# Bounce stores queued one by one behind weight loads, and the leftover tokens' first product with both halves of x side by side

## The chip, the cores and the metric

The kernel runs on 1 core of a Trainium2 chip. The metric is the device time of one execution in microseconds. Before the change the median of 3 runs is 1294.83 us (1294.04 to 1295.26).

The engines are named as in the profile: PE (matrix multiplies; PEld is its weight load), DVE (vector), ACT (scalar), POOL (GpSimd) and SP, which only issues DMAs. All DMAs of this kernel are issued by SP, and its rows in the trace are rows of issuing.

## The reference

A linear-attention layer, then a feed-forward layer, then four dense experts weighted by probabilities, on 2304 tokens of 512 features:

```python
def phi(x):
    proj = np.einsum('bhsd,df->bhsf', x, w_phi)
    proj = proj - np.max(np.abs(proj), axis=-1, keepdims=True)
    return np.concatenate([np.exp(proj), np.exp(-proj)], axis=-1)
q_p, k_p = (phi(q), phi(k))
kv = np.einsum('bhsf,bhsd->bhfd', k_p, v)
z = np.sum(k_p, axis=2)
x = einsum(q_p, kv) / (einsum(q_p, z) + 1e-6)      # 2304 x 512
...
h = x @ w_in                                       # 2048 wide
x = (h * (1.0 / (1.0 + np.exp(-1.702 * h)))) @ w_out
...
p = domain_probs / (domain_probs.sum(-1, keepdims=True) + 1e-09)
for e in range(4):
    out += p[:, e:e + 1] * (np.maximum(x @ w1[e], 0.0) @ w2[e])   # 1024 wide
```

## The kernel before, in words

**Tokens and units.** The tokens are held feature-major in SBUF in two groups: group 0 of 1024 tokens and group 1 of 1280, which is two halves of 512 and a REST of 256 "leftover tokens". Each feed-forward layer is cut into units, each a slab of 256 hidden columns. The list UNITS runs through them: units 0 to 7 are layer 1 on group 0, 8 to 15 layer 1 on group 1, 16 to 31 layer 2 on group 0, 32 to 47 layer 2 on group 1 (these are in LATE). NU is 8. Numbers are split into a high and a low part in a matmul format, and each product takes three matmuls (PASSES): weights high with x high, weights high with x low, weights low with x high.

**A unit.** For the 1024 tokens in halves a unit makes seven block products (steps 0 to 6, function first and products, 6 matmuls of 512 columns each); the second products of the unit before are put between the steps. The PSUM banks 0, 1 and 2 ("a", "b", "c") take the first products: bank 0 from step 0 on, bank 2 from step 5 on. The 256 leftover tokens take no part in the blocks: in units of group 1, rest_first is called after step 3 (its result in bank 2) and after step 5 (in bank 0), and each time plain_rest makes 12 matmuls of 256 columns (4 slices of the features, 3 passes). Then hidden() makes the activation: in layer 1 a tanh gate by ACT (L778), a multiply by DVE (L781), a cast by ACT (L793) and the low part by POOL; in layer 2 a relu by ACT (L797) and the low part by DVE (L798). Over the program plain_rest runs 48 times: 2 times for each of 8 units of layer 1 and 16 of layer 2.

**Two ways in which the order is set.** The attention stage and the units 0 to 8 are one list of words, ORDER, written out by hand; in_order ties each instruction to the one before it on its engine. From unit 9 on a loop over UNITS writes the rest, with background work (generators in the list bg, one step per call) between the steps. SP is not held to ORDER: the scheduler places a DMA where it finds it ready.

**The attention stage, as far as the change touches it.** Each of the 16 pairs of heads takes a maximum over the features; it goes to DRAM (rd1, mx_d, L615) and comes back broadcast to all partitions (rd2, "mb", L620). The subtraction of it (es, L625) and the two exponentials (en L628, ep L631) make the pair's eq, which the matmuls n0 to n2 (L703, 72 rows) read. The key side has exponentials too (kn L670, kp L673), read by the matmuls v0 and v1 (L678, L685). Between them the layer-1 weights, which come as 64-bit numbers, are loaded (h..ld, raws, L266) and converted (abs L338, rb L340, sg L344, cl L346, sh L350, ad L352, mu L354 or L358) and stored to w1_d for the second group (st, L323), from where load() reads them again (L290).

**The probabilities.** They are loaded into pn and normalised (np0, np1; L512 to L517). For units 32 to 47 a row of them is needed along the free axis, so each expert's 1024 values of group 1 are written to pn_d in DRAM (L1356: 128 partitions, 8 values of 4 bytes each) and read back broadcast (row, L314) from unit 32 on. The four stores stand in the loop at unit NU + 2, that is 10, and nothing ties them to a place on SP.

Of the kernel before, what the change touches and what calls it, by code (L numbers as in the profile page):

```python
# [9 lines left out]
F32 = mybir.dt.float32  # L10
F32R = mybir.dt.float32r
# [7 lines left out]
P = 128  # L19
# [4 lines left out]
KC = DM // P  # L24
F1 = 2048 // P
E = 4
F2 = 1024 // P
NG = F1 + E * F2
PASSES = ((0, 0), (0, 1), (1, 0))

HALF = 512
BASE = (0, 1024)
SIZE = (1024, 1280)
REST = SIZE[1] - 2 * HALF
# [9 lines left out]
NU = 8  # L44
# [115 lines left out]
def fused(ctx: ExitStack, tc: tile.TileContext, qT, kT, v, w_phi, wg1, wg2, probs, out):  # L160
    nc = tc.nc
# [33 lines left out]
    def bank(i, n=1):  # L195
        return psa[:, i * 512:(i + n) * 512]

    TAGS = ("a", "b", "c", "acc0", "acc1", "acc2", "acc3", "acc4")
# [9 lines left out]
    pn_d = dram.tile([E, 8, P], F32, name="pn_d")  # L208
# [12 lines left out]
    def low(eng, dst, src, hi):  # L221
        eng.tensor_tensor(out=dst, in0=src, in1=hi.bitcast(F32), op=ALU.subtract)  # L222


    raw64, raw, win, wout = {}, {}, {}, {}
# [12 lines left out]
    late = {}  # L238
# [7 lines left out]
    def third_area():  # L246
        leave("A")
        pool = enter("D")
        for i in (2, 4, 5):
            late["xo%d" % i] = pool.tile([P, 2, 2, HALF], F32R, name="xo%d" % i)  # L250
        late["ss"] = pool.tile([P, 4, 256], F32, name="ss")
        late["xr"] = [pool.tile([P, KC, REST], F32R, name="xr%d" % e) for e in range(2)]
        ring["gr"] = deque(pool.tile([P, 2, REST], F32R, name="gr%d" % i) for i in range(2))
        late["mm"] = pool.tile([P, HALF], F32, name="mm")
        late["uu"] = pool.tile([P, 2, HALF], F32, name="uu")
        late["h"] = pool.tile([P, HALF], F32, name="hs")
        late["id"] = pool.tile([P, P], F32, name="ident_out")
# [55 lines left out]
    def row(e, k):  # L313
        nc.sync.dma_start(  # L314
            out=prow(k), in_=pn_d[e, 4 * k:4 * k + 4].rearrange("t p -> (t p)").rearrange("(o n) -> o n", o=1)
            .to_broadcast([P, HALF])
        )

    def prow(k):
        return late["ss"].rearrange("p (a b) f -> p a (b f)", a=2)[:, k]  # L320
# [111 lines left out]
    xo = {}  # L432
# [50 lines left out]
    def build_rest():  # L483
        xo["rest"] = t = late["xr"]
        src = xv[1][:, :, 2 * HALF:]
        nc.scalar.copy(t[0], src)
        yield
        low(nc.vector, t[1], src, t[0])
        yield

    bg = deque()
# [366 lines left out]
    class Unit:  # L858
# [97 lines left out]
                self.psf[0, 1] = self.c  # L956

        def plain_rest(self, i, ps):
            k_ = 0
            for kc in range(KC):  # L960
                for a, e in PASSES:
                    nc.tensor.matmul(  # L962
                        ps, win[self.u][:, a, 2 * i + kc // 2, (kc % 2) * P:(kc % 2 + 1) * P], xo["rest"][e][:, kc, :],
                        start=(k_ == 0), stop=(k_ == 11),
                    )
                    k_ += 1

        def plain_first(self, i, k, ps):
            n = 0
# [14 lines left out]

        def rest_first(self, i, tag):
            older, self.stages = self.stages, deque()
            ps = bank(TAGS.index(tag))[:, :REST]
            self.plain_rest(i, ps)
            self.g[i, 2], st = hidden(self.layer, ps, REST)
            next(st)  # L990
            self.stages.append(st)
            self.finish(older)
# [136 lines left out]
    def ffn(name, slot, var):  # L1129

        kind = name.rstrip("0123456789.")
        u, *ij = (int(x) for x in name[len(kind):].split("."))
        unit = units.setdefault(u, Unit(u))
        if kind in "PMUBHC":
            unit.strassen_step(kind, *ij, slot)
            return
        i, j = ij
        if kind in "SE":
            if kind == "S":
                unit.sums[i, j] = bank(int(slot[1:]))  # L1140
                unit.plain_second(i, j, unit.sums[i, j])
            else:
                unit.plain_add(i, j, unit.sums[i, j])
        elif kind == "F":
            unit.psf[i, j] = bank(int(slot[1:]))
            if j == 2:
                unit.plain_rest(i, unit.psf[i, j][:, :REST])
            else:
                unit.plain_first(i, j, unit.psf[i, j])
        else:  # L1150
            n = REST if j == 2 else HALF
            src = unit.psf[i, j][:, :n]
            if kind == "Va":
                unit.sg[i, j] = sgs[int(slot)][:, :n]
                gate(unit.sg[i, j], src)
            sg = unit.sg[i, j]
            if kind == "Vb":
                gated(sg, src)
            elif kind == "Ha":
                unit.g[i, j] = ring["gr"][int(slot)] if j == 2 else gs[int(slot)]  # L1160
                nc.scalar.copy(unit.g[i, j][:, 0, :], sg)
            elif kind == "Hb":
                g = unit.g[i, j]
                low(nc.vector if var else nc.gpsimd, g[:, 1, :], sg, g[:, 0, :])
# [151 lines left out]
    for u, (grp, layer, q) in list(enumerate(UNITS))[NU + 1:]:  # L1316
        unit = Unit(u)
        if u + 5 < len(UNITS) and UNITS[u + 5][2] == 0:
            ready = deque(build_x(UNITS[u + 5][0], (3, 6)).values())
        if u + 1 < len(UNITS) and UNITS[u + 1][2] == 0:  # L1320
            while pre:
                pump(pre)
            bx = ready
        if u in LATE:
            if u + 1 < len(UNITS):
                bg.append(load_in(u + 1))
            if u == LATE[0]:
                last_stage()
            else:
                bg.append(chain(before))  # L1330
            if u == LATE[-2]:
                bg.appendleft(gather((4, 7)))
            if u == LATE[-1]:
                bg.append(gather((6, 1), (4, 6), (2, 1)))
            bg.append(prep_out(u))
            if u != LATE[-1]:
                bg.append(prep_sums_out(u))
            bg.append(load(u + 2))
        else:
            if layer == 2:  # L1340
                bg.append(sums_out(u))
            else:
                bg.append(prep_sums(u + 1))
            bg.append(prep_out(u))
            bg.append(load(u + 2))
            if u + 1 in LATE:
                bg.append(load_in(u + 1))
            else:
                if layer == 2:
                    bg.append(prep_sums(u + 1))  # L1350
                bg.append(prep_in(u + 1))
                if UNITS[u + 1][1] == 2:
                    bg.append(store_in(u + 1))
        if u == NU + 2:
            for e in range(E):
                nc.sync.dma_start(out=pn_d[e].rearrange("t p -> p t"), in_=pn[:, BASE[1] // P:BASE[1] // P + 8, e])  # L1356
        if grp and q == 0:
            for _ in build_rest():
                pass
        strassen_unit(unit)  # L1360
        while bg or free:
            background(1)
        unit.finish(unit.stages)
        before = unit
# [54 lines left out]
```

## Time and profile before

| | before |
|---|---|
| median of 3 runs | 1294.83 us |
| the profiled execution | 1290.59 us, of which 1288.8 us lie between its first and last instruction (the span) |
| PE busy | 1259.6 us (98%) |
| PEld, DVE, ACT, POOL busy | 1054.6, 810.8, 538.6, 799.0 us |
| granted TensorE clock, mean | 0.992 of full speed |
| PE busy in 40 slices of the span | 8999999967999999999999999999999999999999 |

A digit of the last row is the busy share of one slice in tenths (9 is 90% or more); a slice is 1288.8 / 40 = 32.2 us long. PE is busy nearly throughout; the slices that fall out are the ninth and the tenth, 258 to 322 us from the start, which is the end of the attention stage. The other engines are idle for a third of the span or more, so that PE is the one to follow.

### The profile page before, as it was taken

The numbers are of one execution on the slowest core, as the hardware profiler recorded it, in microseconds if no ns is written. First come the engines' busy times: TensorE is split into PE (matmuls) and PEld (weight loads), VectorE is DVE, ScalarE is ACT, GpSimd is POOL, SyncE is SP. The second block draws the span as 40 slices with busy tenths as digits, with TensorE's granted clock in tenths as the row PEclk, the third lists the DMA queues.
The fourth block names the chain that finished last, engine by engine and source line by source line (L and its number), as shares of the span: only waits on it lengthen the run. The fifth ranks groups of instructions, "written<-read, shape, count | busy, mean of one in ns | idle before, by whom it ended". The sixth has DMA issues, their size and how long they took to land.

```text
span 1288.8 us, 20442 instructions
## 1 busy us (share of the span) xinstructions
PE 1259.6 (98%) x8181; PEld 1054.6 (82%) x8181; DVE 810.8 (63%) x1243; ACT 538.6 (42%) x826; POOL 799.0 (62%) x617
## 2 busy tenths in 40 slices
PE   8999999967999999999999999999999999999999
PEld 6888878856888888888888888888888888888887
DVE  7887777744844565655544556566466666666675
ACT  6987565644454333542222323233522322322321
POOL 5634343323776775795757567554876886787784
PEclk9999999987999999999999999999999999999999
DMA  7754544354110010244445443555334334423302
GB/s 230 227 167 143 182 157 134 113 89 97 63 66 34 33 66 34 98 164 196 158 186 204 169 200 147 212 212 199 129 132 139 137 116 136 158 104 141 147 1 82
DMA packets 62161, 174.00 MB, mean 135 GB/s; under 512 B 28018, under 2 KB 28402, under 8 KB 55922
## 3 DMA queue, kind: packets, MB, share of 16 engines
q1 hardware_dynamic: 62066, 172.70, 38.6%
q8 instruction: 64, 1.05, 0.3%
q14 instruction: 31, 0.25, 0.1%
HBM read 117.54 MB, written 55.14 MB: 134 GB/s over the span
## 4 chain that ended last, share of the span: by engine, by line
PE 71%; ACT 0%; issue 0%; ACTq 0%
PE psa L873 29%; PE psa L1037 17%; PE psa L1075 11%; PE psa L1035 8%; PE psa L962 5%; PE psa L1116 1%; PE psa L1106 0%; ACT xa L1123 0%; ACTq L1123 0%
## 5 line engine op out<-in xcount | busy, mean ns | idle before, releaser
L873 PE MATMUL psa<-xo,win 128*128 128x512 f32 x1680 | 422.4, 389 | 0.0
L873 PEld LDWEIGHTS psa<-xo,win 128*128 128x128 f32 x1680 | 314.1, 188 | 64.9 <-POOL win L222 0.3
L1037 PE MATMUL psa<-wout,g 128*128 128x512 f32 x768 | 189.7, 389 | 0.0
L222 POOL TENSOR_TENSOR g<-sg,g 128x512 fp32r<-128x512 f32 x85 | 114.0, 1345 | 105.8 <-ACT g L793 53.2
L222 POOL TENSOR_TENSOR wout<-raw,wout 128x1024 fp32r<-128x1024 f32 (+1 forms) x49 | 108.0, 2205 | 103.1 <-ACT wout L413 102.0
L1037 PEld LDWEIGHTS psa<-wout,g 128*128 128x128 f32 x768 | 144.1, 188 | 29.8
L880 DVE TENSOR_TENSOR xa<-psa,xa 128x512 f32<-128x512 f32 x178 | 119.9, 688 | 12.7 <-PE psa L1075 12.7
L1057 DVE SCALAR_TENSOR_TENSOR xa<-psa,pn,xa 128x512 f32<-128x512 f32 x114 | 85.4, 749 | 64.8 <-PE psa L1037 64.7
L222 POOL TENSOR_TENSOR g<-xa,g 128x512 fp32r<-128x512 f32 x69 | 89.2, 1299 | 31.0 <-ACT g L821 30.8
L797 ACT ACTIVATE g<-psa 128x512 fp32r<-128x512 f32 x48 | 28.7, 598 | 180.8 <-DVE psa L880 125.1
L1035 PE MATMUL psa<-g,wout 128*128 128x512 f32 x384 | 95.3, 390 | 0.4 <-DVE xa L1005 0.4
L996 PE MATMUL psa<-g,wout 128*128 128x512 f32 x384 | 92.7, 392 | 0.0
L1075 PE MATMUL psa<-g,ws 128*128 128x512 f32 x360 | 92.2, 391 | 0.0
L973 PE MATMUL psa<-xo,win 128*128 128x512 f32 x384 | 91.8, 391 | 0.0
L880 DVE TENSOR_TENSOR uu<-psa,mm 128x512 f32<-128x512 f32 x80 | 55.1, 688 | 56.3 <-PE psa L873 50.4
L973 PEld LDWEIGHTS psa<-xo,win 128*128 128x128 f32 x384 | 71.6, 188 | 15.6 <-issue 0.6
L996 PEld LDWEIGHTS psa<-g,wout 128*128 128x128 f32 x384 | 71.3, 188 | 15.8 <-DVE eq L625 0.4
L1035 PEld LDWEIGHTS psa<-g,wout 128*128 128x128 f32 x384 | 71.1, 188 | 15.0 <-DVE xa L1005 0.9
L821 ACT CAST g<-xa 128x512 fp32r<-128x512 f32 x72 | 44.7, 621 | 88.6 <-DVE xa L812 43.1
L222 POOL TENSOR_TENSOR win<-raw,win 128x1024 fp32r<-128x1024 f32 (+1 forms) x31 | 67.7, 2185 | 19.1 <-ACT win L427 12.2
L962 PEld LDWEIGHTS psa<-xr,win 128*128 128x128 f32 x576 | 75.4, 191 | 3.7
L962 PE MATMUL psa<-xr,win 128*128 128x256 f32 x576 | 76.6, 283 | 0.0
(161 smaller groups left out, 2161.5 us busy)
## 6 DMA issues: line engine op xcount, KB each, us to landing
wi_d<-win SPq DMA_DIRECT2D x16, 2048.0 KB, 6.3
win<-wi_d SPq DMA_DIRECT2D x16, 2048.0 KB, 8.1
raws<-in_wg_dram SPq DMA_DIRECT2D x32, 512.0 KB, 5.5
raw<-in_wg_dram SPq DMA_DIRECT2D x16, 1024.0 KB, 5.1
w_d<-raw SPq DMA_DIRECT2D x8, 1024.0 KB, 6.6
raw<-w_d SPq DMA_DIRECT2D x8, 1024.0 KB, 4.6
ws_d<-ss SPq DMA_DIRECT2D x16, 512.0 KB, 4.5
raw<-in_wg_dram SPq DMA_DIRECT2D x16, 512.0 KB, 3.2
```

The source lines that it names most:

```text
L222: eng.tensor_tensor(out=dst, in0=src, in1=hi.bitcast(F32), op=ALU.subtract)
L797: nc.scalar.activation(out=hi, in_=src, func=AF.Relu)
L821: nc.scalar.copy(g[:, 0], h)
L873: nc.tensor.matmul(ps, win[self.u][:, a, w, kc * P:(kc + 1) * P], xo[i][:, e, kc, :], start=start and k_ == 0, stop=stop and k_ == 5, skip ...
L880: nc.vector.tensor_tensor(out=out, in0=ps, in1=other, op=ALU.add)
L962: nc.tensor.matmul(ps, win[self.u][:, a, 2 * i + kc // 2, (kc % 2) * P:(kc % 2 + 1) * P], xo["rest"][e][:, kc, :], start=(k_ == 0), stop=( ...
L973: nc.tensor.matmul(ps, win[self.u][:, a, 2 * i + kc // 2, (kc % 2) * P:(kc % 2 + 1) * P], x[:, e, kc % 2, :], start=(n == 0), stop=(n == 11),)
L996: nc.tensor.matmul(ps, wout[self.u][:, a, i, t * P:(t + 1) * P], self.g[i, k][:, e, :], start=(n == 0), stop=(n == 5))
L1035: nc.tensor.matmul(p, w[:, a, i, t_ * P:(t_ + 1) * P], v_, **f)
L1037: nc.tensor.matmul(p, v_[:, t_ * P:(t_ + 1) * P], w[:, a, i, :], **f)
L1057: nc.vector.scalar_tensor_tensor(out=o, in0=ps, scalar=col, in1=o, op0=ALU.mult, op1=ALU.add)
L1075: nc.tensor.matmul(ps, quarter(a), g[:, e, :], start=n == 0 and (m != 5 or first), stop=n == 2 and (m != 5 or final), skip_group_check=True,)
```

## The change

**The bounce stores.** The four stores to pn_d leave the loop body of unit 10. A generator store_row(e) makes one of them and ties it behind the last SP instruction written so far; it is put into bg right behind load(u + 2), so the units 10, 11, 12 and 13 each store one expert's row behind their weight load.

**The leftover tokens.** Both parts of their x become one tile, xr, so that for one slice of the features the high part and the low part (256 columns each, 1024 elements apart) can be one moving operand of 512 columns. plain_rest then makes, for each of 4 slices, one matmul of 512 columns with the high weights and one of 256 with the low weights: 8 matmuls in place of 12, and as many columns. The results lie side by side in a whole bank, and fold() adds them: ACT copies the right 256 columns to SBUF (fold), DVE adds them to the left 256 in place. Unit 8 keeps the 12 matmuls; the other 23 units of group 1 take the new form, 46 times.

```diff
-        late["xr"] = [pool.tile([P, KC, REST], F32R, name="xr%d" % e) for e in range(2)]
+        late["xr"] = pool.tile([P, 2, KC, REST], F32R, name="xr")
+        late["fold"] = pool.tile([P, REST], F32, name="fold")
...
+    def store_row(e):
+
+        traced = nc.cur_bb.bb.instructions
+        behind = next(i for i in reversed(traced) if i.engine == mybir.EngineType.SP).name
+        start = len(traced)
+        nc.sync.dma_start(out=pn_d[e].rearrange("t p -> p t"), in_=pn[:, BASE[1] // P:BASE[1] // P + 8, e])
+        for ins in traced[start:]:
+            tc.add_manual_dep(
+                ins, behind, mybir.DependencyInfo(mybir.DependencyClass.NoSync, mybir.DependencyReason.DATA),
+                reason="step order",
+            )
+        yield
...
         def plain_rest(self, i, ps):
-            k_ = 0
+
+            x, n = xo["rest"], 0
+            if self.u == NU:
...
             for kc in range(KC):
-                for a, e in PASSES:
+                for a, w in ((0, 2 * REST), (1, REST)):
                     nc.tensor.matmul(
-                        ps, win[self.u][:, a, 2 * i + kc // 2, (kc % 2) * P:(kc % 2 + 1) * P], xo["rest"][e][:, kc, :],
-                        start=(k_ == 0), stop=(k_ == 11),
+                        ps[:, :w], win[self.u][:, a, 2 * i + kc // 2, (kc % 2) * P:(kc % 2 + 1) * P],
+                        x[:, :, kc, :] if a == 0 else x[:, 0, kc, :],
+                        start=(n == 0), stop=(n == 2 * KC - 1), skip_group_check=True,
                     )
-                    k_ += 1
+                    n += 1
+
+        def fold(self, ps):
+            nc.scalar.copy(late["fold"], ps[:, REST:])
+            self.add(ps[:, :REST], ps[:, :REST], late["fold"])
+            return ps[:, :REST]
...
         def rest_first(self, i, tag):
             older, self.stages = self.stages, deque()
-            ps = bank(TAGS.index(tag))[:, :REST]
+            ps = bank(TAGS.index(tag))
             self.plain_rest(i, ps)
+            ps = self.fold(ps)
...
             bg.append(load(u + 2))
+            if 0 <= u - NU - 2 < E:
+                bg.append(store_row(u - NU - 2))
...
-        if u == NU + 2:
-            for e in range(E):
-                nc.sync.dma_start(out=pn_d[e].rearrange("t p -> p t"), in_=pn[:, BASE[1] // P:BASE[1] // P + 8, e])
```

The scheduler's order on SP, near the end of the attention stage, before the change: the maximum of the last pair goes out (m to mx_d), comes back broadcast (mx_d to mb), the last two 64-bit weight loads follow (raws), then the stores and loads of layer-1 weights (w_d).

```order
L615 DMA mx_d<-m_123 36x32
L1356 DMA pn_d<-pn 128x8x1
L620 DMA mb_114<-mx_d 128x1152
L1356 DMA pn_d<-pn 128x8x1 x3
L266 DMA raws_0_91<-in_wg_dram 128x512
L266 DMA raws_1_92<-in_wg_dram 128x512
L323 DMA w_d<-raw_140 128x2048
```

And with the change, from the same place on:

```order
L629 DMA mx_d<-m_123 36x32
L634 DMA mb_114<-mx_d 128x1152
L267 DMA raws_0_91<-in_wg_dram 128x512
L267 DMA raws_1_92<-in_wg_dram 128x512
L337 DMA w_d<-raw_140 128x2048
L291 DMA raw_140<-w_d 128x2048
L337 DMA w_d<-raw_141 128x2048
L291 DMA raw_141<-w_d 128x2048
L291 DMA raw_140<-w_d 128x2048
L291 DMA raw_141<-w_d 128x2048
L291 DMA raw_140<-w_d 128x2048
L325 DMA pn_d<-pn 128x8x1
```

Before, one store to pn_d stands ahead of the broadcast that fills mb, and three stand between it and the loads of raws. Now the broadcast and the two loads follow each other directly. The first store to pn_d stands behind the load of unit 12's weights, five loads of raw later; the other three follow in the same way, each behind the load of the next unit's weights (13, 14 and 15).

On DVE, around the second set of leftover tokens in a steady unit of layer 1 (steps 5 and 6). Before (hs is the sum of step 5, sg_102 the gate of the leftover tokens, the xa row the eviction of a second product, the last two the value of step 6):

```order
L880 TENSOR_TENSOR hs<-psa,uu 128x512
L781 SCALAR_TENSOR_TENSOR sg_103<-sg_103,hs 128x512
L781 SCALAR_TENSOR_TENSOR sg_102<-sg_102,psa 128x256
L1049 TENSOR_TENSOR xa_75<-psa,xa_75 128x512
L880 TENSOR_TENSOR psa<-psa,uu 128x512
L781 SCALAR_TENSOR_TENSOR sg_103<-sg_103,psa 128x512
```

With the change:

```order
L894 TENSOR_TENSOR hs<-psa,uu 128x512
L795 SCALAR_TENSOR_TENSOR sg_103<-sg_103,hs 128x512
L894 TENSOR_TENSOR psa<-psa,fold 128x256
L1080 TENSOR_TENSOR xa_75<-psa,xa_75 128x512
L795 SCALAR_TENSOR_TENSOR sg_102<-sg_102,psa 128x256
L894 TENSOR_TENSOR psa<-psa,uu 128x512
L795 SCALAR_TENSOR_TENSOR sg_103<-sg_103,psa 128x512
```

The addition of the fold comes ahead of the eviction, and the last read of bank 0, the multiply of 256 columns into sg_102, moves behind it. On ACT the copy to fold takes the place of the gate of 256 columns, which follows behind the cast of the hs value. Everything before unit 9 stands on PE, ACT, DVE and POOL as before, apart from the names of the xr tiles.

## Rows read from the trace of the kernel before

**Rows 1.** Who PE waited for: engine, line, releaser: us in total, times, longest.

```profile
PE psa L703 <- ACT eq L631: 10.3, 1, 10.3
```

**Rows 2.** PE's timeline, end of attention: start, us, instruction, count, idle before and releaser.

```profile
256.65 0.44 PE L678 MATMUL psa<-v,ek 128*64 128x130 f32 x4
...
259.11 0.28 PE L607 MATMUL psa<-ident,r 128*36 128x128 f32 x1
...
272.65 6.96 PE L996 MATMUL psa<-g,wout 128*128 128x512 f32 x30
289.95 3.91 PE L703 MATMUL psa<-kv,eq 128*64 128x65 f32 x72 [10.34 <-ACT eq L631]
...
303.05 2.00 PE L685 MATMUL psa<-v,ek 128*64 128x65 f32 x32 [8.96 <-ACT ek L673]
...
307.15 0.66 PE L735 MATMUL psa<-ident,on 128*128 128x128 f32 x4
...
308.00 2.32 PE L703 MATMUL psa<-kv,eq 128*64 128x65 f32 x72
```

**Rows 3.** SP's timeline there: start and length of issuing.

```profile
267.29 0.38 SPq L1356 DMA_DIRECT2D pn_d<-pn  x1
267.77 0.52 SPq L620 DMA_DIRECT2D mb<-mx_d  x1
268.33 12.95 SPq L1356 DMA_DIRECT2D pn_d<-pn  x3
281.38 11.73 SPq L266 DMA_DIRECT2D raws<-in_wg_dram  x2
```

**Rows 4.** DVE's timeline there.

```profile
285.09 1.36 DVE L625 TENSOR_TENSOR eq<-eq,mb 128x1152 f32<-128x1152 f32 x1 [12.36 <-DMA mb<-mx_d]
```

**Rows 5.** ACT's timeline there.

```profile
286.48 2.22 ACT L628 ACTIVATE eq<-eq 128x1152 f32<-128x1152 f32 x2 [13.07 <-DVE eq L625]
288.73 1.16 ACT L631 ACTIVATE eq<-eq 128x1152 f32<-128x1152 f32 x1
301.40 0.65 ACT L344 ACTIVATE raws<-raws 128x512 f32<-128x512 f32 x1 [11.51 <-DMA raws<-in_wg_dram]
```

**Rows 6.** DMA issues by line: count, KB each, median us from issue to landing.

```profile
raws<-in_wg_dram SPq DMA_DIRECT2D x32, 512.0 KB, 5.5
...
xa<-mx_d SPq DMA_DIRECT2D x8, 576.0 KB, 4.4
```

**Rows 7.** One stretch: busy time of each engine, granted clock (PEclk), DMA share.

```profile
284.00:286.00 2.00, 0.00 (x0) 0.00 (x0) 0.91 (x1) 0.00 (x0) 0.00 (x0) 0.50 1.01 27
```

**Rows 8.** POOL's timeline, end of attention.

```profile
272.26 1.32 POOL L358 TENSOR_TENSOR raw<-raw,raws 128x512 f32<-128x512 f32 x1 [5.61 <-ACT xa L748]
```

**Rows 9.** PE's timeline in a steady unit of layer 1, group 1.

```profile
435.89 1.60 PE L962 MATMUL psa<-xr,win 128*128 128x256 f32 x12
437.32 1.55 PE L1035 MATMUL psa<-g,wout 128*128 128x512 f32 x6
438.71 2.88 PE L873 MATMUL psa<-xo,win 128*128 128x512 f32 x12
441.43 1.52 PE L1035 MATMUL psa<-g,wout 128*128 128x512 f32 x6
```

**Rows 10.** DVE's timeline there.

```profile
437.54 0.69 DVE L781 SCALAR_TENSOR_TENSOR sg<-sg,hs 128x512 f32<-128x512 f32 x1 [0.76 <-ACT sg L778]
438.15 0.41 DVE L781 SCALAR_TENSOR_TENSOR sg<-sg,psa 128x256 f32<-128x256 f32 x1
438.91 0.69 DVE L1049 TENSOR_TENSOR xa<-psa,xa 128x512 f32<-128x512 f32 x1 [0.35 <-PE psa L1035]
```

**Rows 11.** ACT's timeline there.

```profile
437.60 0.38 ACT L778 ACTIVATE sg<-psa 128x256 f32<-128x256 f32 x1
```

**Rows 12.** SP's timeline, two loads of layer-1 weights in steady units.

```profile
397.87 0.32 SPq L290 DMA_DIRECT2D raw<-w_d  x1
...
424.45 0.32 SPq L290 DMA_DIRECT2D raw<-w_d  x1
```

More of the change, by code (lines that the diff above doesn't have):

```diff
@@ L485, in build_rest @@
         src = xv[1][:, :, 2 * HALF:]
-        nc.scalar.copy(t[0], src)
+        nc.scalar.copy(t[:, 0], src)
         yield
-        low(nc.vector, t[1], src, t[0])
+        low(nc.vector, t[:, 1], src, t[:, 0])
         yield
@@ L958, in plain_rest @@
         def plain_rest(self, i, ps):
-            k_ = 0
+            x, n = xo["rest"], 0
+            if self.u == NU:
+                for kc in range(KC):
+                    for a, e in PASSES:
+                        nc.tensor.matmul(
+                            ps[:, :REST], win[self.u][:, a, 2 * i + kc // 2, (kc % 2) * P:(kc % 2 + 1) * P],
+                            x[:, e, kc, :], start=(n == 0), stop=(n == 11),
+                        )
+                        n += 1
+                return
             for kc in range(KC):
-                for a, e in PASSES:
+                for a, w in ((0, 2 * REST), (1, REST)):
                     nc.tensor.matmul(
-                        ps, win[self.u][:, a, 2 * i + kc // 2, (kc % 2) * P:(kc % 2 + 1) * P], xo["rest"][e][:, kc, :],
-                        start=(k_ == 0), stop=(k_ == 11),
-                    )
-                    k_ += 1
+                        ps[:, :w], win[self.u][:, a, 2 * i + kc // 2, (kc % 2) * P:(kc % 2 + 1) * P],
+                        x[:, :, kc, :] if a == 0 else x[:, 0, kc, :],
+                        start=(n == 0), stop=(n == 2 * KC - 1), skip_group_check=True,
+                    )
+                    n += 1
+        def fold(self, ps):
+            nc.scalar.copy(late["fold"], ps[:, REST:])
+            self.add(ps[:, :REST], ps[:, :REST], late["fold"])
+            return ps[:, :REST]
         def plain_first(self, i, k, ps):
@@ L1146, in ffn @@
             if j == 2:
-                unit.plain_rest(i, unit.psf[i, j][:, :REST])
+                unit.plain_rest(i, unit.psf[i, j])
             else:
```

## The prediction

> **What bounds the kernel now.** I read the page first: PE is busy for 98% of the span, at nearly full clock, so time is gained only where a matmul gets cheaper or where PE waits. Then the view of who PE waited for: its longest entry is one wait of 10.3 us for an exponential on ACT [rows 1]. The timeline of PE shows where: 10.34 us ahead of the n matmuls at 289.95, and a second wait of 8.96 us ahead of the v matmuls at 303.05 [rows 2]. Both lie at the end of the attention stage.
>
> Followed back, the first wait goes: PE waits for the exponentials on ACT, ACT for the subtraction L625 on DVE [rows 5], and DVE stands still for 12.36 us until the DMA that fills mb lands [rows 4]. That DMA was issued at 267.77 [rows 3], so it took 17.3 us to be used at 285.09. The same kind of transfer (xa<-mx_d, as large) lands after 4.4 us in the median [rows 6]. The second wait: ACT stood 11.51 us ahead of the sign L344 for a load of raws [rows 5], and the exponential that PE wants is queued behind that sign. SP shows what both have in common: a store to pn_d was issued 0.48 us ahead of mb, three more right behind it kept SP issuing for 12.95 us, and the two loads of raws behind those took 11.73 us more to get out [rows 3]. These stores move only 4 KB each, but as 1024 values of 4 bytes. So I read both waits as one queue blocked by the stores.
>
> The pause has a second price. At 284 to 286 the granted clock is 0.50 [rows 7], the lower of the two levels (1.2 GHz), and PE had done nothing since 279.6. The 72 n matmuls at 289.95 then take 3.91 us, where the same 72 at 308.00 take 2.32 [rows 2].
>
> **The stores moved: what it is worth.** I rebuild the stretch from the end of the 30 matmuls that start at 272.65 [rows 2]. One matmul of 512 columns goes out every (441.43 - 438.71) / 12 = 0.227 us [rows 9], so PE could go on at 272.65 + 30 x 0.227 = 279.45.
>
> First, is the n group ready by then? With mb issued at 267.77 as before and 4.4 us of landing [rows 6], it is there at 272.2. DVE is free at 285.09 - 12.36 = 272.73 [rows 4]. From the start of L625 to the first exponential are 1.39 us, from there to L631 2.25, and L631 takes 1.16 [rows 4, 5]: 272.73 + 4.80 = 277.5. That is 1.9 us before PE asks, so the first wait is gone.
>
> Second, the v group. The load of raws needs the buffer that POOL frees at 272.26 + 1.32 = 273.6 [rows 8]; with 5.5 us to landing [rows 6] the sign can start at 279.1, and PE was released 303.05 - 301.40 = 1.65 us after that start [rows 2, 5]: 280.75. PE comes there after the n matmuls, at 279.45 + 2.3 = 281.75. The margin is 1.0 us; the second wait is gone too.
>
> Then the stretch takes 2.3 us for n and 259.11 - 256.65 = 2.46 us for v, both as at full clock [rows 2]: 279.45 + 4.8 = 284.2. Before, PE reached the next matmuls (L735) at 307.15 [rows 2]. **Term 1: 22.9 us gained**, of which 19.3 are the two waits and some 3.6 the clock. What follows hangs on the same releases and moves up as a whole. In their new place the stores cost only queue time: loads of layer-1 weights follow each other by 26.6 us [rows 12], and four stores, mb and the loads together were through by 301.4 [rows 3, 5], that is (301.4 - 267.3) / 4 = 8.5 us a store at the most. A store is out of the queue long before the next load comes. Cost 0.
>
> On the order of the queue there is the Trainium skill, "DMA: Bandwidth & Descriptors", section "Two DMAs through the same engine are not ordered": descriptors of one queue start in order. The trace agrees: mb, issued behind one store, was late. [...]
>
> **The leftover tokens: what it is worth.** A set of 12 matmuls of 256 columns takes 437.32 - 435.89 = 1.43 us, 0.119 each [rows 9]. The new set is 4 of 512 and 4 of 256: 4 x 0.227 + 4 x 0.119 = 1.385. The columns are the same; what is saved is what each matmul costs beside its columns, four times. 46 sets give 46 x 0.046 = 2.1 us. The trace has no moving operand of 512 columns in two pieces. If such a matmul cost as much as two of 256 (0.239), nothing would be left; I take the row of 512, since neither a piece boundary nor its cost shows anywhere, and keep 0 to 2.1.
>
> [...] The rows say 13 ns beside the columns at 2.4 GHz (512 / 2.4 = 213 ns of 227). [...]
>
> The fold adds, 46 times, a copy on ACT (like the gate of 256 columns, 0.38 us [rows 11]) and an addition on DVE (like the multiply of 256, 0.41 [rows 10]). Neither engine is the bound. What can be late is bank 0: the next unit's step 0 writes it. Its first matmul stands 6 x 0.227 behind 438.71 [rows 9], at 440.07, or 440.02 with the shorter set. In front of that now come: end of the set 437.44, copy 437.60 to 437.98 [rows 11], DVE's multiply of hs until about 438.15, the fold's addition, the eviction, which starts at 438.91 as before (it waits for PE), 0.61 to the next instruction (437.54 to 438.15), and the multiply of 0.41 [rows 10]: 438.91 + 0.61 + 0.41 = 439.93. It just fits, where before it had 1.5 us. Behind step 3 bank 2 is free until step 5, and in layer 2 more matmuls stand between. I take 0.5 us lost over the seven units of layer 1, from bounds of 0 and 2. **Term 2: 1.6 us gained.**
>
> **The sum.** 22.9 + 1.6 = 24.5 us. On the profiled execution that is 1290.6 - 24.5 = 1266.1. That execution lies 4.2 us under the median of the runs; on the median I get 1294.8 - 24.5 = **1270.3 us**.
>
> **Rivals.**
> 1. *Another wait takes part of the stall's place.* The margin ahead of v is only 1.0 us. If the load of raws took twice as long (11 us), PE would wait 4.5 us, and v would run at the lower clock, 2 us more: 1276.8. If the second wait stayed whole (9.0 us, with the 3.6 of clock), 12.6 us come back: 1282.9. For it: ACT's queue is full of conversions that wait for these loads. Against it: 5.5 is the median with other traffic, and here the queue is empty.
> 2. *The stores are not the cause*, and mb is late for another reason. Then term 2 alone is left: 1293.2. Against it: SP's issuing of 12.95 and 11.73 us [rows 3].
> 3. *Slower:* a moving operand in two pieces streams at a lower rate. At half rate the 184 new matmuls of 512 columns cost 0.227 us more each, 41.8 us, and with term 1 (22.9) the kernel ends 17 us slower by the median, 1312 us. It decides from 24.5 / 184 = 0.133 us more each. No row speaks for it; none shows such an operand either.
>
> **How the numbers follow.** The forecast has a chance of 0.73 (1264 to 1275, with the bounds of the two terms and the 4.2 us between profile and median, should they belong to the stall), rival 1 0.16 (1275 to 1283), rival 2 0.06, rival 3 0.05. The range 1264 to 1281 holds the forecast and most of rival 1. About 0.2% (2.6 us) is what a measurement can tell from no change: rival 2 falls inside it. Faster 0.89, same 0.06, slower 0.05.
>
> **What would show it.** In the profile after, DVE waits for mb under 2 us; PE has no wait above 1 us between the L996 matmuls and L735 and the granted clock stays at full speed there; SP issues one store to pn_d behind each of four loads, 26 us apart, with nothing late behind it; a leftover set takes 1.38 us in 8 matmuls; PE waits for DVE at the start of layer-1 units by some tenths at most. The forecast falls if mb still takes over 10 us to land, if PE waits for ACT ahead of v, or if a set takes more than 1.43 us.

## The result, and the profile after

| | before | with the change |
|---|---|---|
| median | 1295.05 us (1294.04 to 1297.04, 4 runs: the three known before and one more) | 1266.2 us (1265.47 to 1267.56, 4 runs) |
| profiled execution, span | 1290.59, 1288.8 | 1265.47, 1263.7 |
| PE busy | 1259.6 us (98%) | 1252.8 us (99%) |

The ratio is 0.9777, with an interval of 0.976 to 0.9794. Forecast were 1270.3 us and a range of 1264 to 1281. The gain between the two profiled executions is 25.1 us (24.5 forecast), that between the medians 28.9.

SP's timeline of the changed kernel, at the place of [rows 3], at the first weight load that now has a store behind it, and at the next weight load (start of issuing, and the time from the first start to the last end of a merged row):

```profile
266.22 0.33 SPq L634 DMA_DIRECT2D mb<-mx_d  x1
272.63 8.60 SPq L267 DMA_DIRECT2D raws<-in_wg_dram  x2
...
373.75 0.32 SPq L291 DMA_DIRECT2D raw<-w_d  x1
374.12 0.43 SPq L325 DMA_DIRECT2D pn_d<-pn  x1
400.31 0.32 SPq L291 DMA_DIRECT2D raw<-w_d  x1
```

DVE's timeline, at the place of [rows 4]; then ACT's, at that of [rows 5]:

```profile
271.67 2.15 DVE L639 TENSOR_TENSOR eq<-eq,mb 128x1152 f32<-128x1152 f32 x1
```

```profile
273.85 2.22 ACT L642 ACTIVATE eq<-eq 128x1152 f32<-128x1152 f32 x2 [1.42 <-DVE eq L639]
276.11 1.17 ACT L645 ACTIVATE eq<-eq 128x1152 f32<-128x1152 f32 x1
277.18 0.66 ACT L358 ACTIVATE raws<-raws 128x512 f32<-128x512 f32 x1
277.74 1.04 ACT L687 ACTIVATE ek<-ek 128x1024 f32<-128x1024 f32 x1
```

PE's timeline there, the stretch of [rows 2]:

```profile
271.68 6.96 PE L1027 MATMUL psa<-g,wout 128*128 128x512 f32 x30
278.57 2.32 PE L717 MATMUL psa<-kv,eq 128*64 128x65 f32 x72
...
280.94 1.10 PE L699 MATMUL psa<-v,ek 128*64 128x65 f32 x32
...
283.13 0.66 PE L749 MATMUL psa<-ident,on 128*128 128x128 f32 x4
```

And the windows view of that stretch (busy time of PE, PEld, DVE, ACT, POOL; granted clock, DMA share, GB/s):

```profile
271.00:283.00 12.00, 12.00 (x178) 10.44 (x176) 8.01 (x14) 9.03 (x13) 7.25 (x6) 1.00 0.22 66
```

The subtraction that stood 12.36 us for mb stands for nothing, and neither does the sign that stood 11.51 us for raws: no bracket stands behind it. PE goes through without a gap at full clock. From the 30 matmuls to the transposes (L749) it takes 283.13 - 271.68 = 11.45 us, where it took 34.50. The longest wait of PE left in the whole span is 1.7 us, at 31.55, long before. PE reaches the stretch 0.97 us earlier than before. That is no work of the change: nothing ahead of the stretch was changed, and this start moves from run to run (272.28 in e1, 273.17 in e5, which repeats the changed kernel).

PE's timeline in a steady unit of layer 1, the place of [rows 9], and at the last unit of layer 1 (second piece):

```profile
411.73 1.56 PE L986 MATMUL psa<-xr,win 128*128 128x512 f32 x8
413.13 1.55 PE L1066 MATMUL psa<-g,wout 128*128 128x512 f32 x6
414.52 2.93 PE L887 MATMUL psa<-xo,win 128*128 128x512 f32 x12
417.29 1.07 PE L1066 MATMUL psa<-g,wout 128*128 128x512 f32 x4
...
519.49 3.42 PE L887 MATMUL psa<-xo,win 128*128 128x512 f32 x12
522.75 1.52 PE L1066 MATMUL psa<-g,wout 128*128 128x512 f32 x6
```

DVE's timeline in the same unit, the place of [rows 10]:

```profile
413.99 0.42 DVE L894 TENSOR_TENSOR psa<-psa,fold 128x256 f32<-128x256 f32 x1
414.72 0.69 DVE L1080 TENSOR_TENSOR xa<-psa,xa 128x512 f32<-128x512 f32 x1 [0.30 <-PE psa L1066]
415.33 0.41 DVE L795 SCALAR_TENSOR_TENSOR sg<-sg,psa 128x256 f32<-128x256 f32 x1
```

A leftover set takes 413.13 - 411.73 = 1.40 us (1.43 before; 1.385 forecast). The 12 matmuls of step 6 and the next step 0 take 417.29 - 414.52 = 2.77 in place of 2.72: the multiply that frees bank 0 ends at 415.74, and step 0's first matmul would stand at 414.52 + 1.36 = 415.88, so the fit is as tight as forecast. In unit 15 it doesn't fit, and the same twelve take 522.75 - 519.49 = 3.26.

### The profile page after: what moved, and what is told of

The parts are those of the page before. It is cut to its first block, busy times and chain, and to the rows that moved or that the text cites. A ratio compares the mean times of both kernels' runs of the same rounds, so it can differ in the third digit from the quotient of the medians.

```text
span 1263.7 us, 20113 instructions
## 1 busy us (share of the span) xinstructions
PE 1252.8 (99%) x7997; PEld 1039.9 (82%) x7997; DVE 827.5 (65%) x1289; ACT 554.6 (44%) x872; POOL 797.9 (63%) x617
## 4 chain that ended last, share of the span: by engine, by line
PE 72%; DVE 1%; ACT 0%; issue 0%; ACTq 0%; DVEq 0%
PE psa L887 29%; PE psa L1068 17%; PE psa L1106 11%; PE psa L1066 8%; PE psa L986 5%; PE psa L1147 1%; DVE xo L222 0%; PE psa L1137 0%; ACT sg L792 0%; DVE sg L795 0%; DVE xa L1080 0%; DVE psa L894 0%; DVE hs L894 0%; ACT fold L994 0%; ACT xa L1154 0%
## 5 line engine op out<-in xcount | busy, mean ns | idle before, releaser
L894 DVE TENSOR_TENSOR xa<-psa,xa 128x512 f32<-128x512 f32 x178 | 121.1, 687 | 12.7 <-PE psa L1106 12.7
L1106 PEld LDWEIGHTS psa<-g,ws 128*128 128x128 f32 x360 | 65.4, 188 | 13.7
L792 ACT ACTIVATE sg<-psa 128x512 f32<-128x512 f32 (+1 forms) x72 | 39.3, 549 | 79.5 <-PE psa L887 24.5
```

The lines of the kernel that those rows point to most:

```text
L792: nc.scalar.activation(out=out, in_=src, func=AF.Tanh, scale=0.851)
L894: nc.vector.tensor_tensor(out=out, in0=ps, in1=other, op=ALU.add)
L1106: nc.tensor.matmul(ps, quarter(a), g[:, e, :], start=n == 0 and (m != 5 or first), stop=n == 2 and (m != 5 or final), skip_group_check=True,)
```

## The experiments

The runs follow four questions. Each kernel was timed beside the kernel before on the same chip, on four chips in all. The kernel before ran there at 1290.84, 1294.52, 1291.71 and 1293.24 us (medians).

### What each half of the change is worth

**e1_stores_only**: the change without its product; every unit makes the 12 matmuls, and no fold.

```
-            if self.u == NU:
+            if True:
...
-            ps = self.fold(ps)
+            ps = ps[:, :REST]
```

> The four stores moved behind the loads as in the change, the leftover tokens' product as before (12 matmuls of 256 columns, no fold). Theory (the stores in the queue held up mb and raws; moving them is nearly the whole gain): no wait of PE above 1 us between the second products at 272 us and the transposes, a span some 1.1 us above the changed kernel's 1263.7, about 1264.8, and 28 us under before in the timed runs, about 1267.3. Rival (the new product carries a good part): 1275 or more in the timed runs.

**e2_rest_only**: the product with its fold, the stores where they were before.

```
-            if 0 <= u - NU - 2 < E:
-                bg.append(store_row(u - NU - 2))
...
+        if u == NU + 2:
+            for e in range(E):
+                nc.sync.dma_start(out=pn_d[e]..., in_=pn[...])
```

> The leftover tokens' product as in the change, the four stores where they were before. Theory: both waits of PE, 10 us and 9 us, stay; a set takes 1.40 us instead of 1.43, 46 sets give 1.5 us, some tenths go back as waits for bank 0: 1.1 us faster than before, 0.9991 of its time. Rival (the product is worth several us by itself): 0.997 or less.

**e3_before_again**: the kernel before, unchanged.

> The kernel before, unchanged, profiled once more. The profiled execution of before took 1290.6 us, its timed runs 1294 to 1297. Theory: the difference lies in the stall itself, whose length goes by how fast the stores are worked off and so varies between executions; an execution of 1295 us then has the two waits of PE longer by some 4 us together, and everything else as long as before. Rival: the 4 us lie elsewhere (the start, the loads), and the two waits are 10.3 and 9.0 us again.

**e5_after_again**: the changed kernel, unchanged, on the second chip.

> The changed kernel, unchanged, beside the kernel before on one chip and beside the stores-only kernel's times. In the first comparison before took 1295 us and the change saved 28.9, while the two profiles differ by 25.1 and the stores-only kernel saved 22.8 where before took 1290.8. Theory: the change itself always takes about 1266 to 1267 and before varies between sessions with the length of its stall; where before takes 1291 the change saves 24 to 25 (22.8 and 0.7 to 1.1 for the product), ratio 0.981. Rival: the saving is 29 on every chip, ratio 0.978.

Measured, as ratio to the kernel before: e1 1268.06 us, 0.9818 (0.9804 to 0.9833); e2 1290.13 us, 0.9992 (0.9983 to 1.0002); e3 1291.07 us, 1.0005 (0.9995 to 1.0015); e5 1266.99 us, 0.9786 (0.9772 to 0.9801). PE's timeline of e1 in the stretch, then who PE waited for in e2:

```profile
279.17 2.32 PE L717 MATMUL psa<-kv,eq 128*64 128x65 f32 x72
...
281.54 1.10 PE L699 MATMUL psa<-v,ek 128*64 128x65 f32 x32
```

```profile
PE psa L717 <- ACT eq L645: 10.1, 1, 10.1
PE psa L699 <- ACT ek L687: 9.6, 1, 9.6
```

The stores alone give 22.8 us and remove both waits; the product alone leaves both waits whole and gives 0.7 us, which is within its interval of nothing. So nearly all of the gain is the stores. e1 has the tiles of the change, too, and takes 913.7 us from the first leftover set of unit 9 to the end of the span, as the kernel before does; so a mere shift of tiles, which costs so much in e7 below, plays no part here.

Two of these runs did not settle what they were for. e3 was to show an execution of 1295 us, and its profiled one took 1290.46, no longer than the first. e5 repeats the time of the changed kernel, but ran on a chip where the kernel before takes 1294.52, so that it does not show what the change saves where that takes 1291.

### What in a store delays its neighbours

**e4_stores_of_32_bytes**: the stores stay in front, four DMAs of 4 KB each, but from a small copy in which a partition's 8 values stand together: 128 pieces of 32 bytes in place of 1024 of 4. The rows are then read back in another order, so that e4 and e6 leave out the order that the reference wants; the work and the bytes are the same.

```
-    pn_d = dram.tile([E, 8, P], F32, name="pn_d")
+    pn_d = dram.tile([E, P, 8], F32, name="pn_d")
...
+    pn_e = const.tile([P, E, 8], F32, name="pn_e")
...
-                nc.sync.dma_start(out=pn_d[e].rearrange("t p -> p t"), in_=pn[...])
+                nc.sync.dma_start(out=pn_d[e], in_=pn_e[:, e, :])
```

> The kernel before, with the four stores at their old place, but each writing 128 runs of 32 bytes from a small copy of pn in which a partition's 8 values lie together, instead of 1024 values of 4 bytes. The rows that are read back for the last 16 units hold the probabilities in another order than the reference wants. Theory (it is the count of small pieces that blocks the queue): both waits of PE are gone, the span is within 3 us of the stores-only kernel, some 1265 to 1268. Rival (four more DMAs ahead cost by their number, whatever their pieces): a wait of some us stays, 1275 or more. Second rival (the stores are not the cause): 1289 as before.

**e6_32_bytes_no_shift**: the same, with the copy in a tile that the program already has for padding, so that no other tile moves (the edit is against e4).

```
-    pn_e = const.tile([P, E, 8], F32, name="pn_e")
+    pn_e = spare_edge[:, 0:32].rearrange("p (e t) -> p e t", e=E)
```

> The kernel before with the four stores at their old place as 128 runs of 32 bytes, the small copy of pn now in a padding tile that is allocated anyway, so that no other tile moves. The rows that are read back hold the probabilities in another order than the reference wants. In the first form of this run both waits of PE were gone, but matmuls whose moving operand is xo took 0.233 us each instead of 0.227 all through the program. Theory (the copy moved all later tiles by 128 bytes, and that is what slowed those matmuls; the stall goes by the count of pieces): now the whole gain shows, 1267 to 1269, as in the stores-only kernel. Rival (something in the stores or rows slows the matmuls): 1280 again.

**e7_shift_alone**: the kernel before, with a tile of the copy's size (128 bytes a partition) that nothing uses.

```
+    const.tile([P, 32], F32, name="shift")
```

> The kernel before with nothing but an unused tile of 128 bytes a partition ahead of the later tiles. Theory (the place of a moving operand in SBUF sets what its matmuls cost beside their columns): 0.233 us for the matmuls with xo, 10 to 13 us slower than before, ratio 1.008 to 1.010, the two waits as before. Rival: no change, 1.000.

Measured: e4 1280.09 us, 0.9915 (0.9897 to 0.9932); e6 1267.03 us, 0.9787 (0.977 to 0.9803); e7 1306.13 us, 1.0087 (1.0072 to 1.0102). SP's timeline of e6:

```profile
266.55 0.33 SPq L1358 DMA_DIRECT2D pn_d<-edge  x1
266.98 0.37 SPq L622 DMA_DIRECT2D mb<-mx_d  x1
267.39 1.38 SPq L1358 DMA_DIRECT2D pn_d<-edge  x3
272.81 8.61 SPq L266 DMA_DIRECT2D raws<-in_wg_dram  x2
```

The order of the queue is that of before, and so are the bytes; SP issues three stores in 1.38 us where it took 12.95, both waits are gone, and the time is that of the stores moved away. What delays is neither the number of DMAs nor their place in the queue as such, but that each is cut into 1024 pieces of 4 bytes. (Whether their number does it, their size, or that they lie scattered in DRAM, where those of one partition are 512 bytes apart, these runs don't separate.)

e4 has both waits gone as well, but lies 12.0 us above e1 on the same chip, and e7 shows why: a shift of the tiles behind it by 128 bytes makes the kernel before 11.6 us slower. The matmuls get slower all through the program. The largest group of PE by shape, of the kernel before and of e7 (behind the bar: busy us, mean ns):

```profile
L873 PE MATMUL psa<-xo,win 128*128 128x512 f32 x1680 | 422.4, 389 | 0.0
```

```profile
L874 PE MATMUL psa<-xo,win 128*128 128x512 f32 x1680 | 428.6, 393 | 0.0
```

In e4 the same group is at 428.6 us, in e6 at 422.4.

### Where a store costs nothing, and where it does

**e10_stores_behind_raws**: all four stores tied behind the last load of raws (lastld), so ahead of the next loads of weights; the product as before.

```
         if u == NU + 2:
+            start = len(nc.cur_bb.bb.instructions)
             for e in range(E):
                 nc.sync.dma_start(out=pn_d[e]..., in_=pn[...])
+            for ins in nc.cur_bb.bb.instructions[start:]:
+                tc.add_manual_dep(
+                    ins, lastld["n"], ...
```

> The kernel before, with the four stores still in one piece in the attention stage, but tied behind the last load of raws, so that mb and raws go out ahead of them; behind them now stand the loads of the layer-1 weights of units 8 and on. Theory (what stands behind the four stores is late by some 25 to 33 us, whatever it is): both waits of PE at 280 to 303 us are gone, the load of unit 8's weights, which in the changed kernel goes out at 289, lands at 315 to 325 instead of 294, ACT's cast of it (due at 300) blocks ACT, and PE stands 5 to 20 us behind that; total between 1273 and 1289. Rival (only mb and raws have no cover): 1268, as stores-only.

**e11_one_store_ahead**: the kernel before, with one store left ahead of mb, and the other three behind weight loads as in the changed kernel.

```
+            if self.i == 15:
+                store_row(0)
+                name = last_sp()
             nc.sync.dma_start(out=self.mb, in_=row.to_broadcast([P, 2 * S]))
+            if self.i == 15:
+                behind(name)
...
+            if 1 <= u - NU - 2 < E:
+                bg.append(store_later(u - NU - 2))
...
-        if u == NU + 2:
-            for e in range(E):
-                nc.sync.dma_start(out=pn_d[e]..., in_=pn[...])
```

> The kernel before, with one store left ahead of the broadcast that fills mb, where the scheduler had it, and the other three queued behind the weight loads of units 11, 12 and 13. What is open: in the kernel before, mb landed 12.9 us late (17.3 from its issue in place of 4.4), but only one store was issued ahead of it; three were issued right behind it. Where all four stood together behind the loads of raws they were through in about 24 us, 6 us each. Theory A (a queue in order, only what stands ahead delays; then one store alone costs mb those 12.9 us): PE's first wait stays at 8 to 11 us, the second is under 2, some 1277 to 1281 us. Theory B (the DMAs in flight share the rings, so the three behind delay mb too): mb lands some 4 to 8 us late, PE's first wait is 0 to 4 us, the second under 2, some 1266 to 1273 us.

**e12_stores_behind_mb**: the kernel before, with mb ahead of all four stores and the loads of raws behind them.

```
+        if after_row:
+            behind(after_row["n"])
...
             nc.sync.dma_start(out=self.mb, in_=row.to_broadcast([P, 2 * S]))
+            if self.i == 15:
+                for e in range(E):
+                    store_row(e)
+                after_row["n"] = last_sp()
...
-        if u == NU + 2:
-            for e in range(E):
-                nc.sync.dma_start(out=pn_d[e]..., in_=pn[...])
```

> The kernel before, with the broadcast that fills mb issued ahead of all four stores, and the last two loads of raws behind them. Theory A (in order): mb lands some 4.4 us after its issue, PE's first wait is gone and the n matmuls run at full clock in 2.32 us; all of the delay is in front of the v matmuls, which still wait for the loads of raws until about 302, so that the second wait is about 20 us in place of 9 and the time hardly changes: 1289 to 1293 us. Theory B (stores issued behind a transfer delay it too): mb lands late, and a first wait of 4 to 10 us stays, with a second of 9 to 15; the time is the same 1289 to 1295 us. The first wait tells them apart, not the time.

Measured: e10 1275.56 us, 0.9849 (0.9834 to 0.9864); e11 1276.29 us, 0.9871 (0.9855 to 0.9888); e12 1282.58 us, 0.9921 (0.9906 to 0.9936).

e10, SP's timeline, then ACT's:

```profile
283.49 14.01 SPq L1360 DMA_DIRECT2D pn_d<-pn  x4
297.78 0.34 SPq L293 DMA_DIRECT2D raw<-w_d  x1
```

```profile
312.57 1.04 ACT L408 CAST win<-raw 128x1024 fp32r<-128x1024 f32 x1 [11.98 <-DMA raw<-w_d]
```

Attention is free of waits here, but the load of weights behind the stores is used 14.8 us after its issue (these loads land after 4.8 us in the median of the changed kernel's profile), and PE stands 2.6 and 0.7 us at the first leftover set. It is busy for 2.69 of the 6 us from 312 to 318, and the granted clock of the next 6 us is 0.63 of full speed in the mean (1.00 in e1). The kernel takes 8.5 us more than e6 on the same chip, where the stores delay nothing. The theory had the place right and the size wrong: the load is some 10 us late, not 25 to 33, and PE waits 3.3 us for it, not 5 to 20. So the new place is free because nothing stands behind the store for 26 us, not because the stores are cheap.

e11, SP's timeline, DVE's, and PE's:

```profile
267.68 0.38 SPq L324 DMA_DIRECT2D pn_d<-pn  x1
268.38 0.32 SPq L641 DMA_DIRECT2D mb<-mx_d  x1
```

```profile
281.87 1.36 DVE L648 TENSOR_TENSOR eq<-eq,mb 128x1152 f32<-128x1152 f32 x1 [8.77 <-DMA mb<-mx_d]
```

```profile
286.72 3.88 PE L726 MATMUL psa<-kv,eq 128*64 128x65 f32 x72 [6.75 <-ACT eq L654]
```

With one store ahead mb is used 281.87 - 268.38 = 13.49 us after its issue, 9.1 more than the median of 4.4; in the kernel before it was 12.9 us late [rows 3, 4]. PE's wait of 6.75 us lies between the two expectations (8 to 11 by theory A, 0 to 4 by B), and the time just under that of A (1277 to 1281). Theory A is right for the larger part, and theory B for 3.8 us: stores issued behind mb delay it too. The windows view of e11 shows when (the columns as above):

```profile
270.00:278.00 8.00, 8.00 (x37) 6.60 (x37) 2.26 (x5) 3.75 (x8) 1.31 (x1) 1.00 0.03 13
...
280.00:282.00 2.00, 0.00 (x0) 0.00 (x0) 0.13 (x1) 0.00 (x0) 0.00 (x0) 1.00 0.97 396
```

And its DMA packets, first from 268 to 270, then from 270 to 278:

```profile
DMA packets 1040, 0.00 MB, mean 2 GB/s; under 512 B 1040, under 2 KB 1040, under 8 KB 1040
...
DMA packets 22, 0.10 MB, mean 13 GB/s; under 512 B 0, under 2 KB 0, under 8 KB 22
```

The pieces of the store are through by 270. Then the DMA engines do next to nothing for 8 us: 22 packets, 3% busy. Only at 280 does mb flow, at 396 GB/s. In the kernel before the picture is the same up to 278 (24 packets between 270 and 278). There the packets from 270 to 281.12, then those from 281.12 to 285, are:

```profile
DMA packets 1246, 0.59 MB, mean 53 GB/s; under 512 B 1118, under 2 KB 1118, under 8 KB 1246
...
DMA packets 1724, 0.01 MB, mean 2 GB/s; under 512 B 1724, under 2 KB 1724, under 8 KB 1724
```

The 1246 - 1118 = 128 large packets are the whole of mb. So its last packet has started by 281.12, 13.4 us after the issue; in e11, by 281.4, it is 13.0 us. What the stores behind add comes after that: in the kernel before the subtraction starts 4.0 us later, at 285.09, behind small packets alone, and in e11 about 0.5 us later.

e12, PE's timeline and DVE's:

```profile
279.83 2.32 PE L729 MATMUL psa<-kv,eq 128*64 128x65 f32 x72
...
293.88 2.00 PE L711 MATMUL psa<-v,ek 128*64 128x65 f32 x32 [11.50 <-ACT ek L699]
```

```profile
272.94 2.15 DVE L651 TENSOR_TENSOR eq<-eq,mb 128x1152 f32<-128x1152 f32 x1
```

The first of its two loads of raws, in SP's timeline and in the view by tile:

```profile
273.90 3.60 SPq L268 DMA_DIRECT2D raws<-in_wg_dram  x1
...
DMA to landing us min/median/max: 18.2/18.2/18.2
```

For comparison the kernel before, with the merged rows of [rows 3] taken apart: the last of the three stores, the two loads of raws, and the first of them in the view by tile:

```profile
269.43 11.84 SPq L1356 DMA_DIRECT2D pn_d<-pn  x1
281.38 0.52 SPq L266 DMA_DIRECT2D raws<-in_wg_dram  x1
...
292.77 0.34 SPq L266 DMA_DIRECT2D raws<-in_wg_dram  x1
...
DMA to landing us min/median/max: 19.9/19.9/19.9
```

With mb ahead of the stores the first wait is gone and the whole delay stands in front of v, as theory A has it. Its size was wrong: I expected about 20 us of wait and no gain, and it is 11.5 us with a gain of 10.7. With nothing between them SP issues the four stores in 3.66 us (12.95 for three before, 11.84 of them for the last), and the first load of raws goes out at 273.90, when POOL has freed its buffer, in place of 281.38. It lands 18.2 us after its issue all the same (3.4 in e6). So the delay isn't a fixed price a store. One store ahead made mb 9.1 us late (e11); four stores ahead made a load some 10 us late in e10 and, against the median of 5.5 [rows 6], 12.7 here. In the kernel before it fell on two loads, one after the other: on mb, and then on the first load of raws. Why SP stood 11.84 us at the last store there is not shown; it was through at 281.27, just when mb had passed.

### What a leftover set costs

**e8_adjacent_pieces**: the two pieces of the moving operand stand side by side, one run of 2 KB.

```
-        late["xr"] = pool.tile([P, 2, KC, REST], F32R, name="xr")
+        late["xr"] = pool.tile([P, KC, 2, REST], F32R, name="xr").rearrange("p k e n -> p e k n")
```

> The changed kernel with xr laid out so that the high and the low 256 columns of a slice stand next to each other: the moving operand of 512 columns is one run of 2 KB instead of two runs of 1 KB that stand 4 KB apart. Nothing else differs. The leftover set took 1.40 us in the changed kernel where 4 x 0.227 + 4 x 0.119 = 1.385 were forecast. Theory A (the jump between the two pieces costs about 4 ns in each of the four wide matmuls): a set takes 1.385, and over 46 sets the stretch from the first set to the end of the span becomes 0.7 us shorter than 912.4. Theory B (widths that alternate cost it, or each set has a fixed price): 1.40 as before, 912.4. The time by either: 1265 to 1267, so the rows decide, not the time. Rival (a shift of tiles inside SBUF moves the speed of all matmuls): the steps of 12 matmuls would leave 2.72 us too.

**e9_wide_first**: four wide matmuls, then four narrow ones.

```
-            for kc in range(KC):
-                for a, w in ((0, 2 * REST), (1, REST)):
+            for a, w in ((0, 2 * REST), (1, REST)):
+                for kc in range(KC):
```

> The changed kernel with the four matmuls of 512 columns of a set first and the four of 256 behind them, in place of taking turns. Theory B (each change of width costs; there are 8 in a set that takes turns and 2 here): a set takes about 1.39, and the end of the last wide product comes 0.36 us earlier, but the fold still waits for the whole set, so the start of the next unit gains nothing else. Theory A (the jump between the two pieces): 1.40 as in the changed kernel. Fixed price of a set: 1.40. The time by either: 1265 to 1267.

Measured: e8 1267.34 us, 0.9808 (0.9788 to 0.9829); e9 1266.7 us, 0.9813 (0.9795 to 0.983). The times say nothing here, as expected; PE's timeline of e8, then of e9, does:

```profile
405.85 1.56 PE L986 MATMUL psa<-xr,win 128*128 128x512 f32 x8
407.25 2.91 PE L1066 MATMUL psa<-g,wout 128*128 128x512 f32 x12
...
405.72 1.54 PE L986 MATMUL psa<-xr,win 128*128 128x512 f32 x8
407.10 2.91 PE L1066 MATMUL psa<-g,wout 128*128 128x512 f32 x12
```

A set takes 1.38 us in e9 and 1.40 in e8, as in the changed kernel; each of the 46 sets of 8 lies within 0.01 of these. The jump between the pieces costs nothing; taking turns between widths costs some 0.02 us a set. From the first set of 8 to the end of the span e9 is 0.9 us shorter than the changed kernel (911.7 against 912.6, and 912.5 to 912.6 in e2, e5 and e8), which is 46 x 0.02. So theory B holds, and theory A and the fixed price of a set fall. It is 0.07% of the time, and e9 is the better kernel by that much.

## Why the prediction was right, point by point

**The two waits (19.3 us) and the clock (3.6).** Right, as the stretch shows: 34.50 to 11.45 us, 23.05 gained where 22.9 were worked out. The chain was right at each link: mb had landed by 271.67, L645, the last exponential, was through 1.3 us before PE's n matmuls (1.9 forecast), and the sign (L358) ran at 277.18 without a wait (279.1 forecast), so v had more margin than the 1.0 us that I gave it. Rival 1 lived on that margin and fell: its doubled load would have shown as a wait ahead of the sign. Rival 2 fell with e1 and e6.

**The reading "one queue blocked by the stores".** Right in what it predicts, wrong in part in how. SP was held, but at one store, the last (11.84 of the 12.95 us); the issue of one store by itself takes 0.38 us with 1024 pieces and 0.33 with 128 (e11, e6). The 11.73 us that I read as the loads of raws getting out are no such thing: the two went out in 0.52 and 0.34 us, and between them the second waited for POOL to free its buffer. The changed kernel has a row of 8.60 there and loses nothing by it. What made the sign late was the first load: its buffer was free at 273.6, it was issued at 281.38, 7.8 us later, and it landed 19.9 us after that, where I had 5.5. So the greater part of the price falls on the transfers behind the stores, which in e11 stand for 8 us beside nearly idle DMA engines. On the Trainium skill, "DMA: Bandwidth & Descriptors", section "Two DMAs through the same engine are not ordered", that descriptors of one queue of one DMA engine start in order but are pipelined: e12 agrees with the first half, with mb in time ahead of four stores, and the 3.8 us of mb's delay from stores behind it (e11 beside the kernel before) fit the second.

**Stores at cost 0 in their new place.** Right; e1 and the changed kernel show no wait there, and e10 shows the price where that cover is missing. The bound that I gave, 8.5 us a store at the most, was a little low: one store alone delayed its neighbour by 9.1.

**The product (1.6 us).** Right in sign, too large. From the first leftover set of unit 9, the first in the new form, to the end of the span the changed kernel takes 912.6 us, and e1, which differs in the product alone, 913.7. Of these 1.1 us 0.4 lie behind the last set, and e6, with the product as before, is shorter there by as much (913.2 in all), so that the product gives some 0.6. Two terms were off. A set takes 1.400 in place of 1.385 (1.433 before), since widths that take turns cost what the rows of equal widths don't show; 46 sets give 1.5 us in place of 2.1. And bank 0 is late by 0.05 us in five units (10 to 14) and by 0.6 in unit 15, some 0.9 together (0.5 forecast). Rival 3 fell: the operand in two pieces costs what a whole one costs. (The 17 us of that rival are 41.8 - 24.5, with both terms taken off and not term 1 alone.)

**How near the sum came.** The profiled executions differ by 25.1 us, and 24.5 were worked out; that is closer than the terms deserve. 23.05 lie in the stretch and 0.6 in the product. The other 1.4, namely the 0.97 by which PE reaches the stretch earlier and the 0.4 behind the last set, are no work of the change. That they made up for the 1.0 by which the product was too large is luck.

**From the profiled execution to the median: the step that was off.** The sum against the profiled execution gave 1266.1 us; I added the 4.2 us by which that execution lay under the median, and the median came out at 1266.2. So those 4.2 us were no constant of the kernel. The kernels whose stall is gone and whose tiles did not move stay at 1266.2 to 1268.1 us wherever one ran (the changed kernel twice, e1, e6, e8, e9), while the medians of the kernel before lie between 1290.8 and 1295.05; on one chip alone 23 executions of it lie between 1287.78 and 1293.17. e3 and e7 speak for the stall as the place: on the chip with 1290.84 the stretch takes 33.80 us in e3, on that with 1294.52 it takes 37.53 in e7, whose waits are 11.7 and 10.7 us. e7's span is 14.9 us longer than the one of before (1303.7 and 1288.8); without the 3.0 that lie in the stretch it is 11.9, about the 11.6 by which it is slower on its own chip. But e7 differs from before in its tiles too, and no long execution of the kernel before itself was profiled, so that this is supported and not shown. If it holds, it is also why the gain between medians (28.9) is larger than that between the profiles (25.1).

## What to carry to other kernels

Here a DMA of 4 KB in 4-byte pieces held up the next load on its queue by 9 us, though its issue took 0.4 us and its bytes are nothing: look for such a DMA just ahead of a load that someone waits for, and either give it larger pieces or put it where nothing stands behind it for a while. Before reading a merged row of issuing as a busy queue, look at its single DMAs: one may be waiting for its buffer. Sum a forecast against the profiled execution, and before carrying a difference to the median over, ask whether it lies in what the change removes. The saving of 0.033 us a set was worth less than a microsecond in all; two waits of the bottleneck engine were worth over twenty.

## What the runs showed that I had not expected

- An added tile of 128 bytes a partition that nothing uses costs 0.87% (e7, 1306.13 us). The 1680 matmuls of the largest group take 393 ns each in place of 389, without a wait or a lower clock. Two kernels that differ in one small tile can't be compared without such a control.
- The DMA engines stand nearly idle for 8 us behind a store of 1024 pieces whose packets have all passed (e11). The profile shows no cause; it stays open, as does why SP gets four stores in a row out sooner when mb does not stand between them (e12).
- A load can be late though all of its packets have passed: in the kernel before, the last packet of mb started by 281.12, and the subtraction that waited for it at 285.09.
